# A Mamba-2 scan followed by a maxout FFN: blocks of one chunk from all four batches, decay exponents broadcast from DRAM, scan matmuls in array tiles

## The chip, the cores and the metric

The kernel runs on one core of a Trainium2 chip. The metric is the device time of one execution in microseconds; the time before is the median of three runs.

## The reference

```python
# x (4, 8, 768, 32), a (4, 8, 768), B and C (4, 8, 768, 16): batch, head, token, width
log_a = log(clip(a, 1e-6, 1))
for each chunk of 32 tokens:
    cum = cumsum(log_a of the chunk)
    L = exp(cum[i] - cum[j]) where i >= j, else 0
    y = ((C @ B.T) * L) @ x + (C @ state) * exp(cum)
    state = exp(sum(log_a)) * state + sum_j B_j x_j exp(cum[-1] - cum_j)
X = y as (batch * token, head * 32)          # 3072 x 256
h = max(X @ w1, X @ w2, X @ w3)              # 256 -> 768
out = h @ w_out                              # 768 -> 256
```

All inputs of the scan are float32; the weights come as float64. The result does not depend on the length of the chunk, and both kernels use chunks of 128 tokens, six per batch.

## The kernel before

**Units of work.** There are 24 chunks (4 batches by 6 chunks, batch by batch), each with all 8 heads. Four chunks in a row make a block of 512 tokens, and there are six blocks. For a block the FFN runs in pieces: six of `up` (L330 to L345; three weight matrices, two matmuls of 512 columns each, the maximum formed by a ScalarE copy `m` and two VectorE maxima into `h`) and four of `down` (L347 to L360).

**Scan of a chunk, in four steps.** `scan_inputs` (L225) multiplies C and B by decays (`Cd`, `Bd`), transposes B, Cd and C on PE, and writes C by head with zeros elsewhere (`CT`). It also builds `W` on GpSimd: the log decays where k <= i. `scan_decay` (L254) lets PE form the exponents, `lower` times `W` (`d`, L260, two matmuls of 512 columns), takes the exponential on ScalarE (L263) and masks on GpSimd (L264). It also makes the new state from one matmul `A` (L270). `scan_scores` (L281) multiplies B with `CT` (`s`, L286, two matmuls of 512 columns over the full array) and `L` (L289). `scan_out` (L292) adds the state's share (L302, full array) and the chunk's own (L308, eight matmuls in 32-column tiles) and copies to `yT`.

**What one trace row of PE is.** A float32 matmul that isn't a transpose leaves two records in the trace; 48 matmuls `d` are 96 records.

**Order.** The steps of the next block's scan are spread among the FFN pieces of the current one (the loops at L364 to L382). Tile's scheduler then orders each engine's instructions; engines work in order and wait on semaphores. SP's queue loads the raw tensors (L94) and stores results (L359); ScalarE's queue loads the weights (L110). Twelve weight jobs are decoded from float64 by six VectorE passes, two GpSimd passes and one ScalarE pass each (L106 to L145), the first ones ahead of the first `up`. Eight completion semaphores are used in turn by the loads and stores, so an issue also waits for the DMA that used its semaphore before it, as a rule the eighth ahead; this holds before and after the change.

Of the kernel before, what the change touches and what calls it, by code (L numbers as in the profile page):

```python
# [18 lines left out]
def kernel(  # L19
# [30 lines left out]
    NF = DF // P  # L50
    BLK = 512
    CPB = BLK // P
    NBLK = T // BLK
# [12 lines left out]
    raw = ctx.enter_context(tc.tile_pool(name="raw", bufs=5))  # L66
    att = ctx.enter_context(tc.tile_pool(name="att", bufs=2))
    ffn = ctx.enter_context(tc.tile_pool(name="ffn", bufs=2))
    wraw = ctx.enter_context(tc.tile_pool(name="wraw", bufs=3))
    wtmp = ctx.enter_context(tc.tile_pool(name="wtmp", bufs=2))  # L70
    ps = ctx.enter_context(tc.tile_pool(name="ps", bufs=1, space=PSUM))

    def att_bank(shape, name):
        return ps.tile(shape, FP32, tag="att", bufs=3, name=name)
# [11 lines left out]
    chunks = {}  # L86

    def load(n):
        b, c = divmod(n, NC)
        sl = slice(c * P, (c + 1) * P)  # L90
        st = chunks[n] = {}
        for name, src, w in (("B", B, N), ("C", C, N), ("x", x, D)):
            st[name] = raw.tile([P, NH, w], FP32, tag="raw_" + name, name="raw_" + name)
            nc.sync.dma_start(out=st[name], in_=src[b, :, sl, :].rearrange("h s n -> s h n"))  # L94

    for n in range(CPB):
        load(n)
# [8 lines left out]
    def decoded(dst, src):  # L106
        """dst [P, 2, WCOL] float32 from src [P, 2, WCOL * 2] words of float64s, low word first."""
        shape = [P, 2 * WCOL]
        rb = wraw.tile([P, 2, WCOL, 2], U32, tag="rb", name="rb")
        nc.scalar.dma_start(out=rb.rearrange("p k f w -> p k (f w)"), in_=src)  # L110
        lo, hi = (rb.rearrange("p k f w -> p (k f) w")[:, :, j] for j in range(2))

        def temp(dtype, name):
            return wtmp.tile(shape, dtype, tag=name, name=name)

        # power of two, with the sign: below float32's range 0, above it infinite
        e = temp(U32, "w_e")
# [45 lines left out]
    for o in range(0, NF, 2):  # L163
# [6 lines left out]
    ident = const.tile([P, P], FP32, name="ident")  # L170
    make_identity(nc, ident)
    upper = const.tile([P, P], FP32, name="upper")
    make_upper_triangular(nc, upper, 1.0, diag=True)
    lower = const.tile([P, P], FP32, name="lower")
    make_lower_triangular(nc, lower, 1.0, diag=False)
    ones = const.tile([P, P], FP32, name="ones")
    nc.vector.memset(ones, 1.0)
    # hsel[p, h] = 1 where p, as (head, state), is of head h
# [7 lines left out]
        base=N - 1, channel_multiplier=-1)  # L186

# [5 lines left out]
    tp = att_bank([P, 2, R], "la_tp")  # L193
    for w in range(2):
        nc.tensor.transpose(out=tp[:, w], in_=lr[:, w], identity=ident[0:R, 0:R])
    la = const.tile([P, NB, NH, NC], FP32, name="la")
    nc.vector.tensor_copy(
        out=la.rearrange("p b h c -> p (b h c)"), in_=tp.rearrange("p w r -> p (w r)"))

    def decays(tri, name):  # L200
        d = att_bank([P, NB, NH, NC], name + "_ps")
        nc.tensor.matmul(
            out=d.rearrange("p b h c -> p (b h c)"), lhsT=tri,
            rhs=la.rearrange("p b h c -> p (b h c)"), start=True, stop=True)
        e = const.tile([P, NB, NH, NC], FP32, name=name)
        nc.scalar.activation(e, d, AF.Exp)
        return e

    to_i = decays(upper, "to_i")
    from_j = decays(lower, "from_j")  # L210
    whole = decays(ones, "whole")
    picked = const.tile([HN, NB, NC, NH], FP32, name="picked")
    for b in range(NB):
        nc.vector.tensor_tensor(
            out=picked[:, b], in0=whole[:, b].rearrange("p h c -> p c h"),
            in1=hsel.unsqueeze(1).to_broadcast([HN, NC, NH]), op=ALU.mult)
    full = const.tile([HN, NB * NC], FP32, name="full")
    nc.vector.tensor_reduce(
        out=full, in_=picked.rearrange("p b c h -> p (b c) h"), op=ALU.add, axis=AX.X)

# [191 lines left out]
```

## Time and profile before

| quantity | value |
|---|---|
| median of 3 runs | 415.1 us (415.0 to 415.52) |
| span of the profiled execution | 413.1 us |
| PE busy | 385.2 us, 93% |
| VectorE busy | 199.7 us, 48% |
| GpSimd, ScalarE busy | 86.1 and 83.5 us |
| DMA traffic | 16.09 MB in 81635 packets |

The span runs from the first to the last instruction of the profiled execution; the runs' median is 2.0 us longer, which lies outside the span. A busy PE means that matmuls are in flight, not that the array runs at its peak. Engine waits are put down to what released them.

### The profile page before, as it was taken

The page shows a single profiled execution, that of the slowest core. Times are in us where ns is not written, and L with a number is a line of the kernel's source. Part 1 is how long each engine was busy: PE and PEld are TensorE (multiplying, and loading weights), DVE is VectorE, ACT ScalarE, POOL GpSimd, SP SyncE. Part 2 cuts the span into 40 slices and gives each one's busy share as a digit, 9 for nine tenths or more (in the row PEclk, how much of TensorE's full clock was granted, in tenths as well). Part 3 has the DMA queues.
Part 4 walks back from the last instruction along what each step waited for, and adds up shares of the span by engine and source line. Part 5 has one row for each costly group of instructions (what it writes and reads, how often), then busy time and mean ns, then how long its engine had stood idle before and what let it go on. Part 6 is the DMA issues. An engine that isn't in the chain of part 4 may idle for free.

```text
span 413.1 us, 4050 instructions
## 1 busy us (share of the span) xinstructions
PE 385.2 (93%) x1496; PEld 210.0 (51%) x1496; DVE 199.7 (48%) x308; ACT 83.5 (20%) x161; POOL 86.1 (21%) x109
## 2 busy tenths in 40 slices
PE   0779799599999999999999999999999999999996
PEld 0434343246644446754446754446654456754465
DVE  4999999954334364134454334442334452212220
ACT  2323331211222112222112222022221021211101
POOL 3656554612201012201022201022111021000000
PEclk9999999799999999999999999999999999999999
DMA  8963543011121021231020231020110000000001
GB/s 200 179 108 41 131 117 100 9 18 22 43 51 13 2 25 11 49 55 13 2 25 9 44 63 13 1 28 0 40 38 0 0 2 0 25 27 0 0 2 51
DMA packets 81635, 16.09 MB, mean 39 GB/s; under 512 B 75280, under 2 KB 78544, under 8 KB 81616
## 3 DMA queue, kind: packets, MB, share of 16 engines
q1 hardware_dynamic: 78352, 9.54, 15.2%
q10 hardware_dynamic: 3264, 6.29, 4.9%
q8 instruction: 12, 0.20, 0.2%
q14 instruction: 7, 0.06, 0.1%
HBM read 12.68 MB, written 3.15 MB: 38 GB/s over the span
## 4 chain that ended last, share of the span: by engine, by line
PE 81%; DVE 14%; SPq 2%; issue 1%; DMA 1%; ACT 0%; ACTq 0%; DVEq 0%
PE up L337 41%; PE o L352 16%; PE d L260 8%; PE s L286 8%; PE y L308 3%; SPq L94 2%; PE tr L244 2%; PE y L302 2%; PE A L270 2%; DVE w_m L141 2%; DVE M L289 2%; DVE w_p L132 1%; DVE CT L250 1%; DVE w_s L124 1%; DVE w_e L118 1%
## 5 line engine op out<-in xcount | busy, mean ns | idle before, releaser
L337 PE MATMUL up<-yT,w 128*128 128x512 f32 x432 | 192.5, 599 | 1.4 <-DVE h L344 1.0
L337 PEld LDWEIGHTS up<-yT,w 128*128 128x128 f32 x432 | 82.0, 192 | 101.7 <-issue 94.9
L264 POOL TENSOR_SCALAR_AFFINE_SELECT L<-L 128x512 f32<-128x512 f32 x48 | 32.5, 678 | 205.3 <-ACT L L263 205.2
L352 PE MATMUL o<-wo,h 128*128 128x256 f32 x288 | 66.6, 383 | 0.0
L344 DVE TENSOR_TENSOR m<-m,up 128x512 f32<-128x512 f32 x36 | 24.7, 686 | 77.3 <-PE up L337 77.3
L352 PEld LDWEIGHTS o<-wo,h 128*128 128x128 f32 x288 | 53.9, 190 | 11.5 <-issue 4.9
L289 DVE TENSOR_TENSOR M<-s,L 128x512 f32<-128x512 f32 x48 | 32.9, 689 | 42.3 <-PE s L286 42.3
L260 PE MATMUL d<-W,lower 128*128 128x512 f32 x96 | 48.2, 616 | 2.3 <-ACT L L263 1.0
L263 ACT ACTIVATE L<-d 128x512 f32<-128x512 f32 x48 | 28.5, 596 | 89.1 <-PE d L260 85.0
L286 PE MATMUL s<-CT,BCT 128*128 128x512 f32 x96 | 46.1, 601 | 0.0
L342 ACT COPY m<-up 128x512 f32<-128x512 f32 x36 | 21.1, 586 | 108.3 <-PE up L337 101.7
L344 DVE TENSOR_TENSOR h<-m,up 128x512 f32<-128x512 f32 x36 | 24.7, 686 | 30.7 <-PE up L337 30.7
L230 POOL TENSOR_SCALAR_AFFINE_SELECT W<-la 128x1024 f32<-128x1024 f32 x24 | 27.7, 1155 | 42.6 <-PE d L260 41.9
L250 DVE TENSOR_TENSOR CT<-tr,hsel 128x1024 f32<-128x1024 f32 x24 | 29.2, 1218 | 9.4 <-ACT BCT L247 9.4
L260 PEld LDWEIGHTS d<-W,lower 128*128 128x128 f32 x96 | 18.2, 198 | 21.6 <-issue 15.5
L286 PEld LDWEIGHTS s<-CT,BCT 128*128 128x128 f32 x96 | 17.5, 190 | 15.5 <-issue 12.6
L274 DVE TENSOR_TENSOR S<-A,hsel 128x256 f32<-128x256 f32 x20 | 8.4, 422 | 26.8 <-PE A L270 26.8
L308 PE MATMUL y<-M,raw_x 128*32 128x128 f32 x384 | 16.7, 280 | 2.4 <-DVE M L289 2.3
L247 ACT COPY BCT<-tr 128x256 f32<-128x256 f32 x24 | 8.9, 372 | 35.3 <-PE y L302 30.4
L235 DVE TENSOR_TENSOR Cd<-raw_C,to_i 128x128 f32<-128x128 f32 x24 | 11.0, 458 | 7.7 <-PE tr L244 7.7
L302 PEld LDWEIGHTS y<-BCT,S 128*128 128x128 f32 x80 | 11.6, 191 | 5.8 <-issue 5.7
L277 DVE SCALAR_TENSOR_TENSOR S<-S,full 128x256 f32<-128x256 f32 x16 | 14.5, 904 | 0.0
(54 smaller groups left out, 198.6 us busy)
## 6 DMA issues: line engine op xcount, KB each, us to landing
rb<-in_moe_w_dram ACTq DMA_DIRECT2D x9, 512.0 KB, 4.1
raw_x<-in_x_dram SPq DMA_DIRECT2D x24, 128.0 KB, 2.9
out_dram<-ob SPq DMA_DIRECT2D x12, 256.0 KB, 2.1
raw_B<-in_B_dram SPq DMA_DIRECT2D x24, 64.0 KB, 2.4
raw_C<-in_C_dram SPq DMA_DIRECT2D x24, 64.0 KB, 3.0
rb<-in_moe_w_out_dram ACTq DMA_DIRECT2D x3, 512.0 KB, 3.8
a_sb<-in_a_dram SPq DMA_DIRECT2D x1, 96.0 KB, 2.6
```

The source lines that it names most:

```text
L230: nc.gpsimd.affine_select(out=W, in_=la[:, b, :, c].unsqueeze(2).to_broadcast([P, NH, P]), pattern=[[0, NH], [1, P]], compare_op=ALU.is_ge ...
L250: nc.vector.tensor_tensor(out=CT, in0=tr[:, 2].unsqueeze(1).to_broadcast([HN, NH, P]), in1=hsel.unsqueeze(2).to_broadcast([HN, NH, P]), op ...
L260: nc.tensor.matmul(out=d.rearrange("j h i -> j (h i)"), lhsT=lower, rhs=st["W"][:, g:g + 4].rearrange("k h i -> k (h i)"), start=True, sto ...
L263: nc.scalar.activation(L[:, g:g + 4], d, AF.Exp)
L264: nc.gpsimd.affine_select(out=L[:, g:g + 4], in_=L[:, g:g + 4], pattern=[[0, 4], [1, P]], compare_op=ALU.is_ge, fill=0.0, base=0, channel_ ...
L286: nc.tensor.matmul(out=s.rearrange("j h i -> j (h i)"), lhsT=st["T"][:, 0], rhs=st["CT"][:, g:g + 4].rearrange("p h i -> p (h i)"), start= ...
L289: nc.vector.tensor_tensor(out=M[:, g:g + 4], in0=s, in1=st["L"][:, g:g + 4], op=ALU.mult)
L308: nc.tensor.matmul(out=y[q * D:(q + 1) * D, t], lhsT=st["x"][:, h], rhs=st["M"][:, h], start=(c == 0 and t == 0), stop=True, tile_position ...
L337: nc.tensor.matmul(out=p, lhsT=w_sb[i][:, k, f * P:(f + 1) * P], rhs=yT[blk][:, k], start=(k == 0), stop=(k == KD - 1))
L342: nc.scalar.copy(out=m, in_=p)
L344: nc.vector.tensor_tensor(out=m if i == 1 else hT[blk][:, f], in0=m, in1=p, op=ALU.max)
L352: nc.tensor.matmul(out=o[:, t % 2], lhsT=hT[blk][:, f, t * P:(t + 1) * P], rhs=wo_sb[:, f], start=(f == 0), stop=(f == NF - 1), skip_group ...
```

## The change

- **Blocks.** A block is one chunk of 128 tokens from each of the four batches (512 tokens again), so that the scan of a block handles four batches at once, and the state moves from block to block.
- **Decay.** VectorE forms the cumulative sum `cum` of the log decays in rows, SP writes it to a DRAM tile `cums` and reads it back, each row to all 128 partitions (`L`, four DMAs of 512 KB per block) and each head's row to 16 partitions (`E`, eight DMAs). GpSimd masks with -30000, ScalarE takes the exponential head by head with minus cum as bias. The matmuls `d` and the tiles `W` go.
- **Array tiles.** `s` becomes 16 matmuls per block in 32-row tiles with two heads in each; `A` 16 matmuls in 32-column tiles; the state's share of `y` 16 matmuls in tiles of 32 rows by 64 columns.
- **Weights.** All loads go through SP; four VectorE passes per job in place of six, one more on ScalarE.
- **Order.** PE's order is now the order of the code; the other engines are ordered by the scheduler.

```diff
-    BLK = 512
+    BLK = NB * P
...
-        nc.scalar.dma_start(out=rb.rearrange("p k f w -> p k (f w)"), in_=src)
+            nc.sync.dma_start(out=rb.rearrange("p k f w -> p k (f w)"), in_=src)
...
+    for w in range(2):
+        nc.vector.tensor_tensor_scan(
+            out=cum[:, w], data0=keep, data1=lr[:, w], initial=0.0,
+            op0=ALU.mult, op1=ALU.add)
+    cums = dram.tile([NB, NH, NC, P], FP32, name="cums")
+    nc.sync.dma_start(
+        out=cums.rearrange("b h c s -> (b h c) s").rearrange("(w r) s -> r w s", w=2), in_=cum)
...
+    def decay_load(c):
+        Ls[c] = L = att.tile([P, NB, NH, P], FP32, tag="L", name="L")
+        for b in range(NB):
+            nc.sync.dma_start(out=L[:, b], in_=cums[b, :, c, :].partition_broadcast(P))
+        if c > 0:
+            st = blocks[c]
+            st["E"] = E = raw.tile([HN, NB, P], FP32, tag="E", name="E")
+            for h in range(NH):
+                nc.sync.dma_start(
+                    out=E[h * N:(h + 1) * N], in_=cums[:, h, c, :].partition_broadcast(N))
+
+    def decay_exp(c, b, h0):
+        L = Ls[c]
+        for h in range(h0, h0 + NH // 2):
+            nc.scalar.activation(
+                L[:, b, h], L[:, b, h], AF.Exp, bias=ncum[:, b, h, c:c + 1], scale=1.0)
...
+        if c > 0:
+            E = st["E"]
+            nc.scalar.activation(E, E, AF.Exp)
+            st["Cd"] = Cd = att.tile([HN, NB, P], FP32, tag="Cd", name="Cd")
+            nc.vector.tensor_tensor(out=Cd, in0=trC, in1=E, op=ALU.mult)
...
+    def scan_scores(c, b0):
+        st = blocks[c]
+        L = Ls[c]
+        banks = [att_bank([P, 2, 2, P], "s") for _ in range(NP)]
+        for i in range(2):
+            b = b0 + i
+            for r in range(NP):
+                rows = slice(r * PN, (r + 1) * PN)
+                nc.tensor.matmul(
+                    out=banks[r][:, i].rearrange("j g i -> j (g i)"), lhsT=st["BT"][rows, b],
+                    rhs=st["CT"][rows, b].rearrange("p g i -> p (g i)"),
+                    start=(i == 0), stop=True, tile_position=(r * PN, 0), skip_group_check=True)
+        for r in range(NP):
+            M = L[:, b0:b0 + 2, 2 * r:2 * r + 2]
+            nc.vector.tensor_tensor(out=M, in0=banks[r], in1=M, op=ALU.mult)
...
+    order = tc.manual_schedule(engines=tc_pe)
...
+    for c in range(NC):
+        n = c + 1
+        scan = {0: (scan_in, n), 1: (scan_state, n), 2: (scan_scores, n, 0),
+                4: (scan_scores, n, 2), 6: (scan_out, n)}
+        for k, (g, i) in enumerate(pieces):
+            g(c, i)
+            for _ in range(2):
+                decode()
+                fetch()
+            if n < NC and k in scan:
+                scan[k][0](*scan[k][1:])
+            if k == 0 and n + 1 < NC:
+                load(n + 1)
+            if k == 3 and n + 1 < NC:
+                decay_load(n + 1)
+            if 4 <= k < 8 and n + 1 < NC:
+                b = k - 4
+                decay_mask(n + 1, b)
+                for h0 in range(0, NH, NH // 2):
+                    decay_exp(n + 1, b, h0)
```

The start of SP's queue, before: the inputs of the four chunks of block 0, with no weights between them.

```order
L81 DMA a_sb<-in_a_dram 96x2x128
L94 DMA raw_B<-in_B_dram 128x8x16
L94 DMA raw_C<-in_C_dram 128x8x16
L94 DMA raw_x<-in_x_dram 128x8x32
L94 DMA raw_B<-in_B_dram 128x8x16
```

The start of SP's queue after the change (`rb` are the undecoded weights):

```order
L86 DMA a_sb<-in_a_dram 96x2x128
L98 DMA raw_B<-in_B_dram 128x32x16
L98 DMA raw_C<-in_C_dram 128x32x16
L98 DMA raw_x<-in_x_dram 128x32x32
L136 DMA rb<-in_moe_w_dram 128x2x512 x3
L210 DMA cums<-cum 96x2x128
L136 DMA rb<-in_moe_w_dram 128x2x512 x2
L234 DMA L<-cums 128x8x128 x4
L136 DMA rb<-in_moe_w_dram 128x2x512 x4
L98 DMA raw_B<-in_B_dram 128x32x16
L98 DMA raw_C<-in_C_dram 128x32x16
```

The store of `cums` now stands behind the raw tensors and three weights, its broadcast `L` behind two more, and four weights stand between that and the raw tensors of the next block.

VectorE ahead of the first block's output, before, around the products `M` of the last chunk of block 0:

```order
L289 TENSOR_TENSOR M<-s,L 128x512
L129 TENSOR_SCALAR w_p<-w_e 128x512
L289 TENSOR_TENSOR M<-s,L 128x512
L132 TENSOR_TENSOR w_p<-w_p,w_s 128x512
L141 SCALAR_TENSOR_TENSOR w_m<-rb,w_tf 128x512
```

The same place after the change, where the product is written over `L`:

```order
L328 TENSOR_TENSOR L<-s,L 128x2x256 x4
L152 TENSOR_SCALAR w_e<-rb 128x512
L159 TENSOR_SCALAR w_t<-rb 128x512
L152 TENSOR_SCALAR w_e<-rb 128x512
L159 TENSOR_SCALAR w_t<-rb 128x512
L328 TENSOR_TENSOR L<-s,L 128x2x256 x4
```

The first passes on two weights, which need their loads, now stand between the first and the last four products of block 0.

ScalarE in the first FFN block, before (`m` is the copy of an `up` result, `L<-d` the exponential):

```order
L263 ACTIVATE L<-d 128x512
L342 COPY m<-up 128x512
L139 ACTIVATE w_tf<-w_t 128x512
L110 DMA rb<-in_moe_w_dram 128x2x512
L342 COPY m<-up 128x512
```

The same place after the change:

```order
L371 COPY m<-up 128x512
L166 ACTIVATE w_p<-w_e 128x512
L163 ACTIVATE w_tf<-w_t 128x512
L166 ACTIVATE w_p<-w_e 128x512
L276 COPY BT<-trB 128x512
L280 ACTIVATE CT<-trC,parity 128x4x128 x2
L251 ACTIVATE L<-L,ncum 128x128 x32
L283 ACTIVATE E<-E 128x512
L371 COPY m<-up 128x512
```

Between the copies of the first and the second `up` now stand all 32 exponentials of the next block and that of `E`.

## Rows read from the trace of the kernel before

**Rows 1.** The page's busy times: engine, us (share of the span), instructions.

```profile
PE 385.2 (93%) x1496; PEld 210.0 (51%) x1496; DVE 199.7 (48%) x308; ACT 83.5 (20%) x161; POOL 86.1 (21%) x109
```

**Rows 2.** Stretches: us, busy us (instructions) per engine, granted clock, DMA share, GB/s.

```profile
core 0: us, PE busy (x) PEld busy (x) DVE busy (x) ACT busy (x) POOL busy (x), PEclk, DMA share, GB/s
0.00:46.80 46.80, 29.12 (x141) 15.26 (x142) 40.24 (x68) 13.41 (x27) 24.73 (x37) 1.00 0.68 129
46.80:118.20 71.40, 65.44 (x248) 34.98 (x247) 51.13 (x84) 16.34 (x31) 26.27 (x27) 0.95 0.27 60
73.90:79.00 5.10, 0.15 (x2) 0.00 (x0) 5.10 (x9) 1.60 (x3) 2.67 (x3) 0.84 0.01 2
79.50:87.02 7.52, 7.52 (x15) 3.21 (x13) 5.72 (x11) 1.21 (x2) 3.71 (x4) 0.69 0.20 20
180.87:243.57 62.70, 62.70 (x250) 34.44 (x248) 26.92 (x41) 12.35 (x24) 9.30 (x12) 1.00 0.17 26
367.84:413.10 45.26, 41.53 (x120) 22.71 (x120) 8.25 (x12) 4.68 (x8) 0.00 (x0) 0.99 0.03 12
```

**Rows 3.** PE in order of time, first block: start us, us, line, operation.

```profile
46.81 10.46 PE L337 MATMUL up<-yT,w 128*128 128x512 f32 x24
...
79.54 7.64 PE L337 MATMUL up<-yT,w 128*128 128x512 f32 x12
87.02 0.61 PE L302 MATMUL y<-BCT,S 128*128 128x128 f32 x4
```

**Rows 4.** PE in order of time, a middle block.

```profile
192.78 5.32 PE L337 MATMUL up<-yT,w 128*128 128x512 f32 x12
197.94 1.88 PE L286 MATMUL s<-CT,BCT 128*128 128x512 f32 x4
199.65 5.31 PE L337 MATMUL up<-yT,w 128*128 128x512 f32 x12
...
207.06 0.27 PE L244 MATMUL tr<-ident,Cd 128*128 128x128 f32 x1
207.17 0.27 PE L244 MATMUL tr<-ident,raw_C 128*128 128x128 f32 x1
...
225.13 0.61 PE L302 MATMUL y<-BCT,S 128*128 128x128 f32 x4
225.68 0.64 PE L308 MATMUL y<-M,raw_x 128*32 128x128 f32 x16
226.25 2.86 PE L352 MATMUL o<-wo,h 128*128 128x256 f32 x12
```

**Rows 5.** Groups by line: shapes, count, busy us, mean ns, idle before and releasers.

```profile
L289 DVE TENSOR_TENSOR M<-s,L 128x512 f32<-128x512 f32 x48 | 32.9, 689 | 42.3 <-PE s L286 42.3
L263 ACT ACTIVATE L<-d 128x512 f32<-128x512 f32 x48 | 28.5, 596 | 89.1 <-PE d L260 85.0 <-DMA rb<-in_moe_w_out_dram 2.9 <-DVE M L289 1.2
L342 ACT COPY m<-up 128x512 f32<-128x512 f32 x36 | 21.1, 586 | 108.3 <-PE up L337 101.7 <-DVE S L277 5.1 <-DVE w_e L118 1.5
L230 POOL TENSOR_SCALAR_AFFINE_SELECT W<-la 128x1024 f32<-128x1024 f32 x24 | 27.7, 1155 | 42.6 <-PE d L260 41.9 <-DVE la L197 0.6
L247 ACT COPY BCT<-tr 128x256 f32<-128x256 f32 x24 | 8.9, 372 | 35.3 <-PE y L302 30.4 <-PE tr L244 5.0
L135 DVE TENSOR_SCALAR w_t<-rb 128x512 uint32<-128x512 uint32 x12 | 7.5, 626 | 0.0
L118 DVE TENSOR_SCALAR w_e<-rb 128x512 uint32<-128x512 uint32 x12 | 6.3, 527 | 2.5 <-DMA rb<-in_moe_w_dram 2.5
```

**Rows 6.** DMA queues from 0 to 17.2 us: packets, MB, share of 16 engines.

```profile
q1 hardware_dynamic: 12592, 1.14, 54.0%
q10 hardware_dynamic: 1088, 2.10, 38.3%
```

**Rows 7.** DMA queue of SP from 0.8 to 4 us.

```profile
q1 hardware_dynamic: 208, 0.10, 11.1%
```

**Rows 8.** DMA issues of the page: KB each, median us from issue to landing.

```profile
out_dram<-ob SPq DMA_DIRECT2D x12, 256.0 KB, 2.1
```

More of the change, by code (lines that the diff above doesn't have):

```diff
@@ L38 @@
     nc = tc.nc
+    tc_pe = {nc.tensor.engine}
     NB, NH, S, D = x.shape
@@ L84, with load @@
     )
-    chunks = {}
-    def load(n):
-        b, c = divmod(n, NC)
+    blocks = {}
+    def load(c):
         sl = slice(c * P, (c + 1) * P)
-        st = chunks[n] = {}
+        st = blocks[c] = {}
         for name, src, w in (("B", B, N), ("C", C, N), ("x", x, D)):
[L93 to L97, printed above, removed]
+            st[name] = raw.tile([P, BH, w], FP32, tag="raw_" + name, name="raw_" + name)
+            nc.sync.dma_start(
+                out=st[name], in_=src[:, :, sl, :].rearrange("b h s n -> s (b h) n"))
+    load(0)
     w_sb = [const.tile([P, KD, DF], FP32, name="w%d" % i) for i in range(3)]
@@ L170 @@
+    for _ in range(3):
+        fetch()
     ident = const.tile([P, P], FP32, name="ident")
     make_identity(nc, ident)
[L172 to L177, printed above, removed]
     hsel = const.tile([HN, NH], FP32, name="hsel")
@@ L186 @@
         base=N - 1, channel_multiplier=-1)
+    parity = const.tile([HN, 2], FP32, name="parity")
+    nc.vector.tensor_reduce(
+        out=parity, in_=hsel.rearrange("p (r g) -> p g r", g=2), op=ALU.add, axis=AX.X)
+    keep = const.tile([R, P], FP32, name="keep")
+    nc.vector.memset(keep, 1.0)
     nc.vector.tensor_scalar(
@@ L192 @@
     nc.scalar.activation(lr, a_sb, AF.Ln)
-    tp = att_bank([P, 2, R], "la_tp")
+    cum = const.tile([R, 2, P], FP32, name="cum")
     for w in range(2):
[L195 to L207, printed above, removed]
@@ new lines, in scan_out @@
+    def scan_out(c):
+        st = blocks[c]
+        M = Ls[c]
+        yT[c] = ffn.tile([P, KD, BLK], FP32, tag="yT", name="yT")
+        ys = [att_bank([P, NB, P], "y") for _ in range(KD)]
+        if c > 0:
+            Sp = states[c]
+            for b in range(NB):
+                for r in range(NP):
+                    rows = slice(r * PN, (r + 1) * PN)
+                    q = r % 2 * 2 * D
+                    nc.tensor.matmul(
+                        out=ys[r // 2][q:q + 2 * D, b],
+                        lhsT=Sp[rows, b].rearrange("p g d -> p (g d)"), rhs=st["Cd"][rows, b],
+                        start=(b == 0), stop=False, tile_position=(r * PN, q),
+                        skip_group_check=True)
+        for b in range(NB):
+            for h in range(NH):
+                t, q = divmod(h, QH)
@@ L312, in scan_out @@
[L312 to L324 removed]
+            nc.scalar.copy(out=yT[c][:, t], in_=ys[t].rearrange("p b i -> p (b i)"))
     hT = {}
[L328 removed]
@@ L364 @@
[L364 to L381 removed]
+                    out=m if i == 1 else hT[c][:, f], in0=m, in1=p, op=ALU.max)
@@ new lines, in down @@
+    def down(c, u):
+        o = ffn_bank([P, 2, DM], "o")
+        for i in range(2):
+            b = 2 * u + i
+            for f in range(NF):
+                nc.tensor.matmul(
+                    out=o[:, i], lhsT=hT[c][:, f, b * P:(b + 1) * P], rhs=wo_sb[:, f],
+                    start=(f == 0), stop=(f == NF - 1), skip_group_check=True)
+        ob = ffn.tile([P, 2, DM], FP32, tag="ob", bufs=3, name="ob")
+        nc.scalar.copy(out=ob, in_=o)
+        nc.sync.dma_start(
+            out=out.rearrange("(b s) m -> s b m", s=S)[c * P:(c + 1) * P, 2 * u:2 * u + 2],
+            in_=ob)
@@ new lines @@
+    order = tc.manual_schedule(engines=tc_pe)
+    ctx.enter_context(order)
+    decay_load(0)
+    ncum = by_token(cum, "ncum", -1.0)
+    from_j = by_token(fj, "from_j", 1.0)
+    for b in range(NB):
+        decay_mask(0, b)
+        for h0 in range(0, NH, NH // 2):
+            decay_exp(0, b, h0)
+    scan_in(0)
+    for _ in range(3):
+        fetch()
+    scan_state(0)
+    scan_scores(0, 0)
+    scan_scores(0, 2)
+    for _ in range(3):
+        decode()
+        fetch()
+    load(1)
+    decay_load(1)
```

307 lines of the change are left out of this document (128 added, 179 removed).

## Prediction

> **What bounds the kernel now.** I read the busy shares first: the tensor engine (PE) is busy for 93% of the span, VectorE for 48% [rows 1]. Then the stretches: a middle block of 512 tokens lasts 62.7 us with PE busy for all of it, and the last block, which has no scan beside it, has 41.5 us of PE work and 45.3 us to the end of the span [rows 2]. So a block is 41.3 us of FFN (without the last drain of 0.2) and 62.7 - 41.3 = 21.4 us of scan. PE bounds the middle blocks: a scan microsecond taken off PE counts there in full, until another engine is late. Ahead lies a head of 46.8 us until the first `up` [rows 3], with the DMA engines 68% busy and PE only 29.1 us [rows 2].
>
> **PE per block before.** The order of PE's rows shows the price of each kind. Four records of `s` (two matmuls) take 199.65 - 197.94 = 1.71 us [rows 4], 0.428 for a record of 512 columns, and hence 0.214 for 256, 0.107 for 128, 0.053 for 64. A block holds 16 records of `s` and 16 like them of `d`: 6.85 us each. Transposes, `A` and `y` make up the other 7.7.
>
> **PE per block after.** `d` goes: -6.85. What stays, each with its bounds:
> - Eight transposes at 0.11 us (207.17 - 207.06) [rows 4]: 0.9.
> - `y` within a chunk: eight matmuls in 32-column tiles, 16 records of 128 columns, take 226.25 - 225.68 = 0.57 us [rows 4]. One after the other they would take 1.71, four side by side 0.43. So column tiles do run side by side, and a visit to them costs 0.15 for going in and out. 64 records at 0.027: 1.7.
> - `A`, 32 records of 64 columns in 32-column tiles: 0.43 if four run side by side, 0.85 at the 0.027 per record that `y` reaches. I take 0.85, the nearest row.
> - `s`, 32 records of 256 columns in 32-row tiles. No row shows a row tile. Below: four side by side, 32 x 0.214 / 4 = 1.7. Above: no overlap at all, 6.85. In between: each record brings its own weights of 128 columns, and records with such weights follow each other no closer than 0.11 us (the transposes) [rows 4]; 32 x 0.11 = 3.5. I take 2.6, midway between side by side and that pace.
> - `y` from the state, 32 records of 128 columns in 32-row, 64-column tiles: 0.86 to 1.7, 3.4 with no overlap. I take 1.3.
> - Five visits to tiles at 0.15: 0.7.
>
> Sum 8.0 us, where the favourable ends give 6.3, the slow weights 9.3 and no overlap 15.2. The period becomes 41.3 + 8.0 = 49.3 us, four times.
>
> A rule speaks for the slow end: the Trainium skill (TensorE: Matmul & The Clock Gate, LDWEIGHTS) says that a weight load takes its time by columns and not by rows, so that 32 rows by 128 columns load no faster than a full array. By that rule `s` takes 3.5 us and the period is 50.6; by rows that run side by side it is 47.6. The 0.11 us between transposes, with 128 weight columns each, agree with it for a full array [rows 4]; no row loads 32 rows.
>
> **Cover in the middle blocks.** The exponentials move to one head each: 32 per block on ScalarE. A 512-column one takes 596 ns, a 256-column copy 372 [rows 5]; the slope gives 0.27 us at 128 columns, so 8.6 us, and with eight 512-column passes and six `m` copies at 0.59 beside them about 17 of 49 us. VectorE loses `CT`, `Cd`, `Bd` in small pieces and keeps 12 maxima and 8 `M` products at 0.69 [rows 5]: 15 us. GpSimd gets four masks of 1.16 [rows 5], `Bd` and the state: about 8. The DMA engines: 12288 packets of 64 to 128 bytes at 11.8 ns (54% of 16 x 17.2 us over 12592) [rows 6] are 9.1 us on 16 engines, as before; new are 4096 packets of 512 bytes for `L`. The rows of the first 3.2 us hold 208 packets, most of them such: 11.1% x 16 x 3.2 / 208 = 27 ns [rows 7], so 7.0 us, and 0.9 for `E`. About 19 of 49 us. Nothing here is late: each `L` is loaded a block ahead. I cost all of it at nothing; it would cost once the loads of a block pass 49 us.
>
> **The head.** Now the decay takes a round trip through DRAM, and one queue (SP's) carries everything. Ahead of `cums` stand block 0's raw tensors and three weights. Before, the same raw bytes and four weights took 17.2 us of nearly full DMA [rows 6]; a weight is 272 packets of 97 ns on 16 engines, 1.65 us. So `cums` moves at 15.5 and lands at 17.4, given the 2.1 us of a store [rows 8]. Two weights are ahead of `L`: 18.8. Four parts of `L`, 7.0: 25.8, landed by 26.3. Mask and exponentials of the last part end at 29.6. VectorE is later: in its order, `w_e` and `w_t` of two weights stand ahead of the last four `M` products, and these weights are queued behind `L`: landed by 30.0, then 1.2 us [rows 5], then 4 x 0.69: 34.0. The last `y` and the first `yT` copy: 36.0 for the first `up`, where 46.8 stands before. VectorE is spared two of six passes per weight, which is why decoding does not hold this longer.
>
> **Block 0.** It has 41.3 us of FFN and 8.0 of scan, of which `A` is hidden in a wait: 7.2. PE has idled in the head; after the wait at 73.9 to 79.0 twelve records of `up` took 87.02 - 79.54 = 7.5 us in place of 5.16 at a granted clock of 0.69 (between the levels of 1.2 and 2.4 GHz) [rows 2 to 4]. I charge this twice, 4.7. Then a new wait. ScalarE's order puts all 32 exponentials of the next block and `E` ahead of the `m` copy of the second `up`, and VectorE puts `Cd`, which needs `E`, ahead of its maxima. DMA: four weights to 32.4, raw tensors to 41.5, `L` to 49.0, the last piece of `E`, whose issue waits for the eighth DMA ahead of it, a part of `L`, 51.1. Mask 50.2, eight exponentials 52.3, `E` 52.9, copy 53.5. PE is at 36.0 + 7.5 + 1.1 + 5.2 = 49.7: it waits 3.8 us. The next `L` holds the fourth `m` copy in the same way, 1.2 us by the same count (68.8 against 67.6). Block 0: 41.3 + 7.2 + 4.7 + 5.0 = 58.2, where 71.4 stands before [rows 2].
>
> **The sum.** 36.0 + 58.2 + 4 x 49.3 + 45.3 = 336.7 us of span against 413.1. The runs' median is 2.0 above the span, which I keep: 339.
>
> **Rivals.**
> - Weight loads one after another, as worked out above: 9.3 per scan, 5 x 1.3 = 6.5 more: 345. For it: the 0.14 us per record of `y` from the state now (0.55 for four, 225.13 to 225.68), where the stream needs 0.107 [rows 4]. Against it: `y` in column tiles, near its stream's rate. Chance 0.20.
> - Row tiles that do not overlap, so that the change does not do what it says on PE: 15.2 per scan, 36 more: 375. Column tiles speak against it, nothing shows rows. Chance 0.07.
> - Reading the same eight rows of `cums` for 128 partitions at half rate: 7 us more for each of the first three `L`, all on the path of the head and of block 0, hidden afterwards: 360. No row of before reads the same bytes again and again. Chance 0.13.
> - The other side: these reads bind the whole kernel. Until the last `L` lands the rest of the queue takes about 94 us (the head's 17, nine weights 15, five sets of raw tensors 46, `E` with its gaps 10, stores 6), and what follows it 75 (30 left of block 4, then 45); with 2 us outside the span and T for each of six `L` the time is 171 + 6T. It is slower than before from T = 41 us, 5.8 times the 7.0 of the row's rate; at 7 times, 49 us, the time is 465. Against it: the packet prices by size lie near one line (12, 27, 97 ns for about 90, 512 and 2048 bytes) [rows 6, 7]. Chance 0.04.
>
> **How the numbers follow.** The forecast keeps 0.56. Its own bounds: the scans between 6.3 and 9.3 (-8 to +7), the head 4 either way, block 0's waits gone or doubled (-5 to +5): 325 to 353. To leave out no more than 2 in 10 the range takes in the half-rate reads: 322 to 364; row tiles without overlap (0.07), bound reads (0.04) and some misjudged start (0.07) are left out. All cases but the last rival are faster: 0.95, same 0.01, slower 0.04, with 0.2% as what a measurement can tell.
>
> **What would show it.** Right: first `up` near 36 us; a middle block near 49 with PE busy throughout; `s` rows spaced under 0.11 us; waits on `E` or `L` only in block 0. Wrong: `L` parts far over 1.75 us each; `s` rows 0.2 apart; `m` copies late behind exponentials in later blocks.

## The result and the profile after

The changed kernel takes **342.4 us** (median of four runs, 342.15 to 343.07) against 415.3: ratio 0.825, 95% interval 0.8236 to 0.8264. 339 was predicted, with a range of 322 to 364. The profiled execution took 342.15, its span is 340.4. Executions of one kernel can fall into two groups some per cent apart, the longer ones at a lower granted clock; ratios are those of the shorter ones.

The page's span and busy times after; the line of PE answers to [rows 1]:

```profile
span 340.4 us, 4340 instructions
PE 300.3 (88%) x1668; PEld 172.0 (51%) x1668; DVE 123.4 (36%) x185; ACT 119.3 (35%) x303; POOL 64.9 (19%) x70
```

PE has 85 us less to do and still ends the span. Where the 73 us went is read from the stretches, with the columns of [rows 2]: head, block 0, the idle time and the cold `up` in it, the first middle block, the block without a next state, the last block.

```profile
0.00:40.76 40.76, 14.14 (x141) 9.93 (x141) 26.93 (x44) 22.47 (x55) 21.43 (x28) 1.00 1.08 236
40.76:101.54 60.78, 51.17 (x289) 28.73 (x289) 31.55 (x43) 32.91 (x90) 25.90 (x25) 0.92 0.75 143
52.70:62.40 9.70, 0.09 (x9) 0.01 (x1) 0.92 (x2) 9.64 (x32) 2.75 (x4) 0.72 1.21 164
62.40:70.09 7.69, 7.69 (x12) 3.13 (x13) 7.61 (x11) 2.89 (x5) 5.53 (x6) 0.69 1.16 304
101.54:150.12 48.58, 48.58 (x290) 27.78 (x289) 14.27 (x22) 17.25 (x46) 6.77 (x7) 1.00 0.44 82
247.27:295.07 47.80, 47.80 (x257) 27.37 (x256) 13.92 (x21) 7.52 (x13) 0.00 (x0) 1.00 0.04 12
295.07:340.40 45.33, 41.42 (x121) 22.61 (x119) 8.26 (x12) 5.28 (x9) 0.00 (x0) 1.00 0.05 18
```

| stretch, us | before | predicted | after |
|---|---|---|---|
| head, to the first `up` | 46.8 | 36.0 | 40.8 |
| block 0 | 71.4 | 58.2 | 60.8 |
| blocks 1 to 4, sum | 249.6 | 197.2 | 193.5 |
| last block | 45.3 | 45.3 | 45.3 |

The sum of blocks 1 to 4 before is 413.1 less the other rows; after, three blocks take 48.58 each and the fourth 47.80. So 56 of the 73 us come from the middle blocks, 17 from the start.

PE in order of time in a middle block after, the counterpart of [rows 4]:

```profile
106.69 0.60 PE L271 MATMUL trB<-ident,raw_B 128*128 128x128 f32 x4
...
112.81 0.65 PE L295 MATMUL A<-raw_x,Bd 128*32 128x64 f32 x32
113.39 5.42 PE L366 MATMUL up<-yT,w 128*128 128x512 f32 x12
118.74 1.15 PE L322 MATMUL s<-CT,BT 32*128 32x256 f32 x16
119.82 10.57 PE L366 MATMUL up<-yT,w 128*128 128x512 f32 x24
...
141.92 1.10 PE L341 MATMUL y<-Cd,S 32*64 32x128 f32 x32
142.95 1.96 PE L349 MATMUL y<-L,raw_x 128*32 128x128 f32 x64
144.83 5.45 PE L381 MATMUL o<-wo,h 128*128 128x256 f32 x24
```

From one start to the next, 16 records of `s` take 1.08 us (0.067 each), twice a block; `y` from the state takes 1.03, `y` within the chunk 1.88, `A` 0.58.

Two stretches of ScalarE in order of time after, the end of the head and the wait in block 0:

```profile
27.78 2.45 ACT L251 ACTIVATE L<-L,ncum 128x128 f32<-128x128 f32 x8
30.98 7.12 ACT L251 ACTIVATE L<-L,ncum 128x128 f32<-128x128 f32 x24 [0.76 <-POOL L L244]
...
51.91 9.45 ACT L251 ACTIVATE L<-L,ncum 128x128 f32<-128x128 f32 x32 [3.27 <-POOL L L244]
61.26 0.61 ACT L283 ACTIVATE E<-E 128x512 f32<-128x512 f32 x1
61.78 0.56 ACT L371 COPY m<-up 128x512 f32<-128x512 f32 x1
```

The third `up` starts at 62.40, when the `m` copy of the second has been made. That copy stands behind 32 exponentials and `E` of the next chunk. VectorE's last four products of the head:

```profile
36.44 2.48 DVE L328 TENSOR_TENSOR L<-s,L 128x512 f32<-128x512 f32 x4 [0.44 <-issue]
```

GpSimd, in the same stretches:

```profile
23.14 1.41 POOL L174 TENSOR_TENSOR w<-w_m,w_p 128x512 f32<-128x512 f32 x1 [0.62 <-DVE w_m L172]
25.61 0.91 POOL L155 TENSOR_SCALAR w_e<-w_e 128x512 uint32<-128x512 uint32 x1 [1.05 <-DVE w_e L152]
26.59 1.16 POOL L244 TENSOR_SCALAR_AFFINE_SELECT L<-L 128x1024 f32<-128x1024 f32 x1
27.71 1.73 POOL L174 TENSOR_TENSOR w<-w_m,w_p 128x512 f32<-128x512 f32 x1
...
49.54 1.29 POOL L174 TENSOR_TENSOR w<-w_m,w_p 128x512 f32<-128x512 f32 x1 [1.23 <-DVE w_m L172]
50.79 4.21 POOL L244 TENSOR_SCALAR_AFFINE_SELECT L<-L 128x1024 f32<-128x1024 f32 x4
```

SyncE's issues of `L`, of chunk 0 and then of chunk 1 (count, shortest, median and longest issue in ns, first and last start), and their times to landing:

```profile
L234 SPq DMA_DIRECT2D L<-cums x4: 367/1027/2188, 15.9 to 18.5; - x4
...
DMA to landing us min/median/max: 4.9/6.9/8.0
...
L234 SPq DMA_DIRECT2D L<-cums x4: 861/1990/2611, 35.0 to 40.8; - x4
...
DMA to landing us min/median/max: 7.1/7.9/8.0
```

Of chunk 0 the first part is on the chip at 15.9 + 4.9 = 20.8 and the last at 18.5 + 8.0 = 26.5, but the first mask starts at 26.59. Of chunk 1 the first part is there at 35.0 + 8.0 = 43.0 at the latest, the last at 48.8, but no mask starts before 50.79. Both times GpSimd's queue has passes on weights ahead of the masks, and these passes wait for VectorE's decoding.

### The profile page after: what moved, and what is told of

Same layout as the page of the kernel before. It is cut to its first block, busy times and chain, and to the rows that moved or that the text cites. A ratio compares the mean times of both kernels' runs of the same rounds, so it can differ in the third digit from the quotient of the medians.

```text
span 340.4 us, 4340 instructions
## 1 busy us (share of the span) xinstructions
PE 300.3 (88%) x1668; PEld 172.0 (51%) x1668; DVE 123.4 (36%) x185; ACT 119.3 (35%) x303; POOL 64.9 (19%) x70
## 4 chain that ended last, share of the span: by engine, by line
PE 81%; SPq 7%; DMA 4%; ACT 3%; DVE 2%; issue 1%; POOL 0%; ACTq 0%; POOLq 0%
PE up L366 53%; PE o L381 19%; SPq L98 5%; PE s L322 3%; PE y L349 3%; ACT L L251 3%; DMA L<-cums 2%; SPq L234 2%; PE y L341 2%; DMA rb<-in_moe_w_dram 1%; SPq L136 1%; DVE w_p L168 1%; DVE w_e L152 1%; DVE w_m L172 1%; DMA E<-cums 1%
## 5 line engine op out<-in xcount | busy, mean ns | idle before, releaser
L366 PE MATMUL up<-yT,w 128*128 128x512 f32 x432 | 193.5, 602 | 10.1 <-ACT m L371 9.6
L251 ACT ACTIVATE L<-L,ncum 128x128 f32<-128x128 f32 x192 | 57.7, 390 | 8.4 <-POOL L L244 8.4
L244 POOL TENSOR_SCALAR_AFFINE_SELECT L<-L 128x1024 f32<-128x1024 f32 x24 | 26.6, 1119 | 98.5 <-DMA L<-cums 98.4
L322 PE MATMUL s<-CT,BT 32*128 32x256 f32 x192 | 17.6, 446 | 17.0 <-DVE L L328 17.0
L328 DVE TENSOR_TENSOR L<-s,L 128x512 f32<-128x512 f32 x48 | 29.8, 684 | 6.0 <-PE s L322 3.8
L322 PEld LDWEIGHTS s<-CT,BT 32*128 32x128 f32 x192 | 11.4, 206 | 26.3 <-DVE L L328 17.7
L168 DVE SCALAR_TENSOR_TENSOR w_p<-rb,w_p 128x512 uint32<-128x512 uint32 x12 | 15.0, 1252 | 0.5 <-ACT w_p L166 0.4
L349 PE MATMUL y<-L,raw_x 128*32 128x128 f32 x384 | 13.5, 296 | 0.8 <-DVE L L328 0.8
L174 POOL TENSOR_TENSOR w<-w_m,w_p 128x512 f32<-128x512 f32 x9 | 12.9, 1429 | 7.0 <-DVE w_p L168 5.0
L349 PEld LDWEIGHTS y<-L,raw_x 128*32 128x32 f32 x384 | 11.3, 119 | 2.9 <-DVE L L328 1.3
L172 DVE SCALAR_TENSOR_TENSOR w_m<-rb,w_tf 128x512 f32<-128x512 uint32 x12 | 10.5, 876 | 0.0
L285 DVE TENSOR_TENSOR Cd<-trC,E 128x512 f32<-128x512 f32 x5 | 3.5, 692 | 19.2 <-ACT CT L280 10.6
```

Source lines behind the costliest of these rows:

```text
L168: nc.vector.scalar_tensor_tensor(out=power, in0=hi, scalar=0x80000000, in1=power, op0=ALU.bitwise_and, op1=ALU.bitwise_or)
L172: nc.vector.scalar_tensor_tensor(out=mant, in0=lo, scalar=2.0 ** -52, in1=topf, op0=ALU.mult, op1=ALU.add)
L244: nc.gpsimd.affine_select(out=L[:, b], in_=L[:, b], pattern=[[0, NH], [1, P]], compare_op=ALU.is_ge, fill=MASKED, base=0, channel_multipli ...
L251: nc.scalar.activation(L[:, b, h], L[:, b, h], AF.Exp, bias=ncum[:, b, h, c:c + 1], scale=1.0)
L322: nc.tensor.matmul(out=banks[r][:, i].rearrange("j g i -> j (g i)"), lhsT=st["BT"][rows, b], rhs=st["CT"][rows, b].rearrange("p g i -> p ( ...
L328: nc.vector.tensor_tensor(out=M, in0=banks[r], in1=M, op=ALU.mult)
```

## The experiments

**Theory:** the middle blocks are bound by PE and shortened by tiles and by the missing `d`; what the start lost against the prediction (4.8 us in the head, 2.6 in block 0) are places in the queues of ScalarE and GpSimd. **Rivals:** the transfers or VectorE's decoding set the start, or the row tiles save nothing.

**Block 0's order alone.**

```diff
-    for b in range(NB):
-        decay_mask(1, b)
-        for h0 in range(0, NH, NH // 2):
-            decay_exp(1, b, h0)
...
+            if c == 0 and k == 1:
+                scan_cd(1)
...
+            if c == 0 and k in (1, 2):
+                for b in (2 * k - 2, 2 * k - 1):
+                    decay_mask(1, b)
+                    for h0 in range(0, NH, NH // 2):
+                        decay_exp(1, b, h0)
```

> Order alone: block 0's exponentials of chunk 1 are written after its second and third up, E and Cd of chunk 1 after the second. Theory 'queue order' (the 9.6 us before the third up come from the m copy standing behind 32 exponentials and E on ScalarE): the third up waits at most 2 us and runs at full clock, 12 us go, of which 2 to 6 may come back as waits before s or on maxima behind decoding: 332 to 336 us against 342.4. Rival 'transfers': the last parts of L and E land at 48.7 and 50.8 whatever the order, and what follows them (masks, 9.5 us of exponentials, products) ends as late as before, so the wait moves to s or y of chunk 1: 340 to 343 us.

Measured: 336.7 us, ratio to before 0.8106 (0.8086 to 0.8125). ScalarE now takes the copies between the exponentials:

```profile
52.06 0.99 ACT L251 ACTIVATE L<-L,ncum 128x128 f32<-128x128 f32 x3 [2.85 <-POOL L L244]
52.95 0.56 ACT L378 COPY m<-up 128x512 f32<-128x512 f32 x1
53.42 5.36 ACT L251 ACTIVATE L<-L,ncum 128x128 f32<-128x128 f32 x18
58.69 0.57 ACT L378 COPY m<-up 128x512 f32<-128x512 f32 x1
```

Block 0 goes from 60.8 to 54.9 us with the same transfers and the same work. So the wait of 9.6 us was a place in ScalarE's queue. Part of it comes back: PE waits 0.49 for `m`, 2.30 for a maximum and 1.70 before the first `down`, somewhat more than was allowed for, so that the time stands 0.7 above the expected range. For block 0 the transfers' rival falls.

**`L` by matmul again.**

```diff
-            nc.sync.dma_start(out=L[:, b], in_=cums[b, :, c, :].partition_broadcast(P))
...
+        nc.gpsimd.affine_select(
+            out=W, in_=la[:, b, :, c].unsqueeze(2).to_broadcast([P, NH, P]),
+            pattern=[[0, NH], [1, P]], compare_op=ALU.is_ge, fill=0.0,
+            base=0, channel_multiplier=-1)
...
+        nc.tensor.matmul(
+            out=d.rearrange("j h i -> j (h i)"), lhsT=lower,
+            rhs=Ws[c, b][:, h0:h0 + 4].rearrange("k h i -> k (h i)"), start=True, stop=True)
+        nc.scalar.activation(L[:, b, h0:h0 + 4], d, AF.Exp)
+        nc.gpsimd.affine_select(
+            out=L[:, b, h0:h0 + 4], in_=L[:, b, h0:h0 + 4], pattern=[[0, 4], [1, P]],
+            compare_op=ALU.is_ge, fill=0.0, base=0, channel_multiplier=-1)
...
-    scan_out(0)
     for b in range(NB):
         decay_mask(1, b)
         for h0 in range(0, NH, NH // 2):
             decay_exp(1, b, h0)
+    scan_out(0)
```

> The broadcast alone undone: L comes from eight 512-column matmuls per block with the lower triangle, eight 512-column exponentials and masks behind them; E still comes through DRAM, tiles and chunks stay. Theory of the prediction: d costs PE 6.85 us in each of four blocks, a middle block goes from 48.6 to 55.4 us, +27.4; the head loses 7 us of transfers and 32 short exponentials, so the first up comes at 33 to 37 in place of 40.8, and block 0's wait of 9.6 and its cold up go, -12: 342.4 + 27.4 - 6 - 12 = 352, range 348 to 358. Rival 'd is free': PE has slack in a middle block, the period stays under 50 us: 325 to 330. Rival 'the head is bound by decoding, not by L': first up at 40 or later, wait stays: 366 to 370.

Measured: 378.8 us (three of four executions; the fourth took 425.7), ratio 0.9115 (0.9092 to 0.9137), above every expectation. The stretches are head, block 0 and a middle block; the rows under them are GpSimd's costliest groups in the head.

```profile
0.00:55.18 55.18, 31.66 (x172) 15.25 (x172) 35.84 (x50) 23.45 (x43) 40.35 (x51) 0.81 0.84 161
55.18:116.75 61.57, 57.80 (x305) 31.29 (x305) 27.36 (x38) 16.94 (x30) 26.15 (x27) 0.97 0.31 48
116.75:172.24 55.49, 55.49 (x306) 30.74 (x304) 14.26 (x22) 12.93 (x22) 11.45 (x15) 1.00 0.23 34
```

```profile
L261 POOL TENSOR_SCALAR_AFFINE_SELECT L<-L 128x512 f32<-128x512 f32 x16 | 13.3, 842 | 1.6 <-ACT L L260 1.4
L249 POOL TENSOR_SCALAR_AFFINE_SELECT W<-la 128x1024 f32<-128x1024 f32 x8 | 9.5, 1194 | 2.9 <-DVE la L226 2.5 <-PE d L257 0.3
```

The middle block is right to 0.1 us: 55.49 against 48.58, so `d` costs 6.91 where 6.85 was computed. The head is wrong by 20 and block 0 by 6 (61.6, where 60.8 + 6.85 - 12 = 55.6 was expected). In the head, two chunks of `W` and of masks (22.8 us) and the weights (8.3 and 6.3 for products and `w_e`) fill GpSimd, 40.35 of 55.18. I had reckoned with the transfers that go and not with the selects that come. But half of the selects are those of chunk 1, and this run also writes chunk 1's `d` ahead of `scan_out(0)` in PE's order:

```profile
39.44 8.28 PE L257 MATMUL d<-W,lower 128*128 128x512 f32 x12
...
50.06 1.95 PE L360 MATMUL y<-L,raw_x 128*32 128x128 f32 x64
```

From 39.44 to 50.06 PE's queue is held by that `d`, with the first block's `y` behind it. So the 14.4 us by which the head is longer than the changed kernel's are in part this run's own order. What the broadcast is worth there is not shown; shown are the 6.9 us a block on PE, 20.7 in blocks 1 to 3.

**One row tile.** Every `s` reads the first 32 rows of its operands in the first tile.

```diff
-                    out=banks[r][:, i].rearrange("j g i -> j (g i)"), lhsT=st["BT"][rows, b],
-                    rhs=st["CT"][rows, b].rearrange("p g i -> p (g i)"),
-                    start=(i == 0), stop=True, tile_position=(r * PN, 0), skip_group_check=True)
+                    out=banks[r][:, i].rearrange("j g i -> j (g i)"), lhsT=st["BT"][0:PN, b],
+                    rhs=st["CT"][0:PN, b].rearrange("p g i -> p (g i)"),
+                    start=(i == 0), stop=True, tile_position=(0, 0), skip_group_check=True)
```

> Every s matmul reads the first 32 rows of its operands and uses the first row tile, so scores of the other heads are not computed (those of the first pair stand in their place); number, shapes and order of the matmuls stay. Theory 'row tiles run side by side': 32 records of 256 columns take 32 x 0.214 = 6.85 us per block in place of 2.15, +4.7 in each of blocks 0 to 4, the head's hidden: 342.4 + 19 to 24 = 361 to 366. Rival 'a 32-row matmul is short by itself': no change, 342. Rival 'only the weight loads overlap': records at about 0.11 us, +1.4 per block: 348 to 350.

Measured: 379.3 us as the median of four (three from 379.1 to 380.5, the shortest 373.2), more than expected. PE in order of time in a middle block of the profiled execution (it took 379.5), then the stretch of these 16 with the columns of [rows 2]:

```profile
127.13 3.72 PE L322 MATMUL s<-CT,BT 32*128 32x256 f32 x16
130.78 12.26 PE L366 MATMUL up<-yT,w 128*128 128x512 f32 x24
```

```profile
127.13:130.85 3.72, 3.72 (x18) 2.96 (x17) 1.88 (x3) 0.63 (x1) 0.00 (x0) 1.00 0.00 0
```

16 records in one tile take 3.65 us from start to start, 0.228 each, at a granted clock of 1.00, and in four tiles 1.08: a gain of 3.4 times, 5.1 us a block and 25.7 in blocks 0 to 4. That makes 368. The shortest execution took 5 us more, and what these are is not shown, since the kept trace is of another.

**The same tiles in another order.** The loops over `r` and `i` in `scan_scores` change places, so that two matmuls of one row tile follow each other.

```diff
-        for i in range(2):
-            b = b0 + i
-            for r in range(NP):
+        for r in range(NP):
+            for i in range(2):
+                b = b0 + i
```

> The same s matmuls in another order: two batches in one row tile after another, then the next row tile. By the run with one row tile a record takes 0.232 us alone and 0.072 in turns over four tiles. Theory 'neighbours overlap only when they are in different row tiles': two of four run side by side, 16 records in about 1.9 us in place of 1.15, +1.5 in each of blocks 0 to 4: 349 to 350. Rival 'the order does not matter, the array keeps four going': 342 to 343. Rival 'no overlap at all across a change of tile': 16 records in 3.7, 355 or more.

Measured: 343.2 us, ratio 0.8256 (0.8232 to 0.828), no difference from the changed kernel's; 16 records take 1.10 from start to start (119.89 to 120.99):

```profile
119.89 1.17 PE L322 MATMUL s<-CT,BT 32*128 32x256 f32 x16
120.99 1.55 PE L366 MATMUL up<-yT,w 128*128 128x512 f32 x3
```

So two matmuls (four records) of one row tile in a row do not lengthen the 16, and strict turns over the tiles are not needed. The first theory falls, its first rival holds.

**`L` twice.** The load of each part of chunks 3 to 5 stands in a loop of two.

```diff
-            nc.sync.dma_start(out=L[:, b], in_=cums[b, :, c, :].partition_broadcast(P))
+            for _ in range(2 if c > 2 else 1):
+                nc.sync.dma_start(out=L[:, b], in_=cums[b, :, c, :].partition_broadcast(P))
```

> Each part of L is loaded twice for chunks 3 to 5 (blocks 1 to 3), the head and block 0 unchanged: 7 us more of DMA in a block of 48.6 whose DMA share is 0.44. Theory 'hidden': L is loaded a block ahead, middle blocks stay at 48.6, 342.4 within 0.7. Rival 'the broadcast contends with the other transfers or with the engines' reads': a middle block grows by 2 us or more, 348 or more.

Measured: 344.2 us, ratio 0.8286 (0.8269 to 0.8304). Blocks 1 to 3 take 49.08, 49.51 and 48.94, 1.8 more in all, and the first `up` comes 0.8 later, at 41.6. Twelve more transfers of half a megabyte are nearly hidden, though not within the 0.7 us that was allowed; the rival's 2 us a block do not show.

**Earlier transfers, three ways.** First, `cums` and the first `L` on ScalarE's DMA queue:

```diff
-    nc.sync.dma_start(
+    nc.scalar.dma_start(
         out=cums.rearrange("b h c s -> (b h c) s").rearrange("(w r) s -> r w s", w=2), in_=cum)
...
+            q = nc.scalar if c == 0 else nc.sync
+            q.dma_start(out=L[:, b], in_=cums[b, :, c, :].partition_broadcast(P))
```

> cums and the four parts of the first L alone go on ScalarE's DMA queue. Theory 'queue order': the parts land some 6 us earlier, but GpSimd and ScalarE take the work in an order that changes with it: the next chunk's exponentials come ahead of the yT copies, so the first up comes no earlier (43 to 47), and the wait in block 0 shrinks by about as much: 337 to 345. Rival 'the head ends with its transfers': first up at 35, wait as before: 336.

Measured: 348.3 us, ratio 0.8379 (0.8347 to 0.841), slower than the changed kernel: the first `up` comes at 49.9. The transfers did not come earlier as a whole. The first part lands at 7.4 + 6.6 = 14.0, but the last at 11.8 + 16.3 = 28.1, where it was 26.5 in the changed kernel, and GpSimd waits for it:

```profile
23.56 1.09 POOL L245 TENSOR_SCALAR_AFFINE_SELECT L<-L 128x1024 f32<-128x1024 f32 x1 [2.74 <-DMA L<-cums]
28.17 1.09 POOL L245 TENSOR_SCALAR_AFFINE_SELECT L<-L 128x1024 f32<-128x1024 f32 x1 [3.52 <-DMA L<-cums]
```

ScalarE's order changed more than was foreseen, too: `BT` and `CT` now stand behind all 32 exponentials, so the first `s` waits for `CT` until 33.4. Second, with the order of block 0 beside it (the first and second diff together):

> The early broadcast and the order of block 0 together, the engines' order otherwise left to the scheduler. Theory 'queue order': 19 exponentials of chunk 1 still stand ahead of the yT copies (9 us of ScalarE with the weights between), so the first up comes near 42, block 0 as in the run with its order alone (54.9): 335 to 340. Rival 'the gains add up' (the parts land 6 us earlier and the first up with them): 330 or 331.

Measured: 350.8 us, ratio 0.8436 (0.84 to 0.8473); first `up` at 49.5, block 0 58.5: worse than both theories, the gains do not add up. Here the last part lands at 10.6 + 17.8 = 28.4. Third, everything in a written order, on all engines:

```diff
+    tc_pe = {e.engine for e in (nc.tensor, nc.scalar, nc.vector, nc.gpsimd, nc.sync)}
...
+        q = nc.scalar if c == 0 else nc.sync
...
+                if 1 <= k < 5:
+                    decay(1, k - 1)
```

> All five engines follow an order written out: cums and the first L go on ScalarE's queue ahead of most weights, only three weights are made before the first up, each mask and its eight exponentials of the first L follow its part, the exponentials of chunk 1 go eight at a time behind the m copies, each weight is made in two stages so that no engine waits inside it. Theory 'queue order' (the head's extra 5 us and the 9.6 us are both places in a queue, not transfers or work): first L landed by about 20, first up at 29 to 33, no wait over 2 us in block 0, middle blocks 48.6 as before: 342.4 - 8 to 12 - 10 = 318 to 325. Rival 'transfers': head and block 0 together are bound by 54 us of DMA for what comes before the first down, so the wait only moves: 332 or more. Rival 'VectorE': decoding (3.4 us a weight), maxima and products take about 46 us of block 0's 50, so up waits for maxima there: 325 to 332.

Measured: 374.6 us, ratio 0.9015 (0.8987 to 0.9044); first `up` at 49.7, block 0 82, where 318 to 325 us were expected. Two reasons can be read. ScalarE in order of time:

```profile
8.85 14.53 ACTq L247 DMA_DIRECT2D L<-cums  x4
23.42 0.58 ACT L296 COPY BT<-trB 128x512 f32<-128x512 f32 x1 [17.82 <-DMA raw_x<-in_x_dram]
```

The four issues hold ScalarE for 14.5 us, and nothing behind them in its queue runs. They start at 8.9, 9.3, 12.9 and 23.0 and take 0.4 to 0.6 us each; the rest is waiting for a completion semaphore that an earlier transfer still has: the third for a weight that lands at 12.9, the fourth for `raw_x`, issued at 9.4 and landed 13.6 us later, at 23.0. The last part so lands at 23.0 + 6.2 = 29.2. And in block 0 the stages of a weight wait for one another through four engines that each follow a written order, with `m` copies and maxima behind them: PE waits five times, 19.6 us in all, for `m`. In none of the three runs does the last part of the first `L` land earlier than in the changed kernel, so none of them shows what earlier transfers would give.

**Only the order of the loads.** No transfer leaves SyncE; that queue is written out, the engines that compute stay with the scheduler. The order of block 0 from the first experiment is in it too, and `A`, `E` and `Cd` of chunk 1 come behind later `up` pieces.

```diff
+    tc_pe = {nc.tensor.engine, nc.sync.engine}
...
+    load(0, "BC")
...
+    fetch()
...
     nc.sync.dma_start(
         out=cums.rearrange("b h c s -> (b h c) s").rearrange("(w r) s -> r w s", w=2), in_=cum)
+    fetch()
+    fetch()
...
+    decay_load(0)
+    load(0, "x")
```

> No DMA leaves SyncE's queue; only its order is written out, and the places of a few steps beside the order of block 0: one weight ahead of cums, two more ahead of the first L, raw_x and the second three weights behind it; in block 0 L of chunk 1 ahead of the third three weights, its A after the fourth up, E and Cd after the fifth. VectorE, ScalarE and GpSimd stay with the scheduler, which now puts three weights in place of five ahead of the first 32 exponentials and none between them and the yT copies. Theory 'queue order' (head): first L landed by 20, its exponentials done by 31, first up at 33 to 35 in place of 40.8, block 0 50 to 55: 323 to 331 us. Rival 'the head cannot be shortened by order': first up at 39 or later, 335 to 338. Rival 'given back in block 0': first up at 33 to 35, but weights and products late there, block 0 at 58 or more: 333 to 338.

Measured: 340.2 us (median of six, 338.0 to 343.7), ratio 0.8163 (0.8141 to 0.8185), where 323 to 331 were expected. In this run `A` of chunk 1 takes the bank from which `Cd` is still to be made, so values of `Cd` differ; number and shapes of the instructions stay. The head comes out as the theory has it, first `up` at 32.7. Block 0 takes 56.4, where 50 to 55 were expected, and blocks 1 to 3 lose 5.5, 2.5 and 2.9 us, which no theory had. In block 1 ScalarE waits 7.76 us for masks and then holds the `m` copy behind 25 exponentials, since `L` now lands too late there. With that mended (`Cd` first, `L` right behind the raw tensors, ScalarE and GpSimd in written order from block 1 on):

```diff
-            if k == 3 and n + 1 < NC:
+            if k == min(c, 1) ^ 1 and n + 1 < NC:
                 decay_load(n + 1)
...
+        if c == 1:
+            ctx.enter_context(tc.manual_schedule(
+                engines={nc.scalar.engine, nc.gpsimd.engine}))
```

> The run before with three repairs: Cd of chunk 1 ahead of its A, the next chunks' L on SyncE's queue right behind their raw tensors (there they came behind three ups and ScalarE's exponentials, ahead of m copies, waited for them: blocks 1 and 2 took 54.1 and 51.0), and from block 1 on ScalarE and GpSimd in written order, eight exponentials behind each of the fifth m copy to the second output copy. Theory 'queue order': first up 32.7 as there, block 0 56.4 as there (VectorE near full with decoding, maxima and products), blocks 1 to 3 48.6, then 47.8 and 45.3, 1.8 outside the span: 32.7 + 56.4 + 145.7 + 47.8 + 45.3 + 1.8 = 330, range 327 to 333. Rival 'the loads of a block no longer fit beside it': blocks 1 to 3 stay above 50.5: 336 or more.

Measured: **329.4 us**, ratio 0.7935 (0.792 to 0.795), the fastest of all. The profiled execution took 332.07. GpSimd's first mask, ScalarE at the end of its head, then the stretches from the first `up`:

```profile
17.65 1.42 POOL L247 TENSOR_SCALAR_AFFINE_SELECT L<-L 128x1024 f32<-128x1024 f32 x1
...
19.11 2.45 ACT L254 ACTIVATE L<-L,ncum 128x128 f32<-128x128 f32 x8 [0.76 <-POOL L L247]
22.91 7.12 ACT L254 ACTIVATE L<-L,ncum 128x128 f32<-128x128 f32 x24 [1.35 <-POOL L L247]
```

```profile
33.27:91.40 58.13, 53.19 (x289) 29.54 (x289) 38.07 (x54) 36.05 (x96) 30.69 (x29) 0.94 0.76 168
91.40:139.98 48.58, 48.58 (x290) 27.79 (x289) 14.26 (x22) 14.93 (x38) 6.77 (x7) 1.00 0.43 82
```

The first exponential starts 8.7 us earlier than in the changed kernel, and the first `up` comes 7.5 us earlier. Two things do this together. The first part of `L` lands at 10.8 + 5.2 = 16.0, 4.8 us earlier; and its mask starts 1.6 us behind that, where it was 5.8 in the changed kernel, since fewer passes on weights stand ahead of it on GpSimd. No run moves one without the other. The middle blocks are untouched.

## Why the prediction was right

- **PE bounds the middle blocks: right.** PE is busy for all of 48.58 us; 49.3 was predicted. `d` was 6.91 for 6.85. `s`, taken at 2.6 between bounds of 1.7 and 6.85, is 2.16, `y` from the state 1.03 for 1.3, `A` 0.58 for 0.85 (nearer to four side by side), the eight transposes 0.87 for 0.9, `y` 1.88 for 1.7. The FFN parts around the five visits take 0.8 more than the 41.3 us, where 0.7 was charged. The errors nearly cancel.
- **The rule on weight loads:** had loads of 128 columns kept records 0.11 us apart, `s` would have taken 3.5; at 0.067 the trace speaks against that reading for different row tiles. The row that the prediction took it from could not show such a pace: the 0.11 us between transposes is also what their 128 streamed columns take (0.107 by its own price). The Trainium skill (TensorE: Matmul & The Clock Gate, Measured speedup vs the span model) gives 3.07 times for four row tiles of 32 rows and 512 columns; the run with one tile gives 3.65 / 1.08 = 3.4 here, with 256 columns. The slow-load rival and the one without overlap both fall.
- **Cover: right.** VectorE 14.3, ScalarE 17.3, GpSimd 6.8 of 48.6, DMA share 0.44; 15, 17, 8 and 0.39 (19 of 49) were predicted, and `L` twice costs 0.4 to 0.9 a block.
- **The transfers of the head: right.** The first `L` is issued from 15.9 to 18.5 and landed within 8.0 us, by 26.5; 26.3 was predicted. No slow reading of the same rows, so these two rivals fall as well.
- **The rest of the head: the step that failed is "Mask and exponentials of the last part end at 29.6".** It let the exponentials run as the parts land. The parts do land from 20.8 to 26.5, but GpSimd has passes on weights ahead of the first mask (26.59) and puts a weight's product between two masks: the first eight exponentials start at 27.78, the others at 30.98, and all end at 38.1. With masks on time they would end near 31.5 by an estimate from the trace: the first part's at 22.0, then 32 exponentials at 0.297 us (7.12 / 24), which is slower than the parts land. The last product ends at 38.9, where "34.0" stands, and the first `up` follows 1.9 later, as the 2.0 of the text. VectorE's weights, named there as what is late, did not hold the products: they waited for masks and exponentials. But GpSimd's passes ahead of the masks wait for VectorE's decoding in their turn, so as a rival decoding is not ruled out here. The last run's first `up` at 33.3 shows that order sets the head, SyncE's and GpSimd's together; how much is GpSimd's alone is read from the traces and not shown by a run.
- **Block 0: right in kind, wrong in size.** The wait stands where it was put, behind 32 exponentials and `E` on ScalarE, and the `up` behind it is cold (7.69 at 0.69). But "Mask 50.2, eight exponentials 52.3" again took 24 of 32 exponentials as done by then: with every mask late they end at 61.3, so the wait is 9.6 and not 3.8. The first `up` (5.3 us) was not cold, -2.35; [rows 3] had the first `up` of before at 10.46 us for 24 records, not cold either. The second wait did not come, -1.2.

In sum: head +4.8, block 0 +2.6, middle blocks -3.7: 340.4 of span against 336.7. That the total is right to 1% is in part luck, since these errors, and those within block 0, have both signs; what was right in kind is the bound on the middle blocks, the cover and the transfers.

## What to carry to other kernels

When transfers replace matmuls, follow the landed data through every in-order queue: who masks it, what stands ahead of it there, and whose copy stands behind it. The landing time was right to 0.2 us and still the stage ended 5 us later. When a test run puts a removed step back, ask also where that step now stands on the other engines (here GpSimd's selects and PE's own order in the head), or the run measures its order as well. And leave the issue of large transfers to an engine that computes nothing: an issue that waits for an earlier transfer's semaphore holds all the work behind it.

## What the runs showed that I had not expected

- Four `L` issues held ScalarE 14.5 us, nearly all of it waiting for earlier transfers to land, and 6.23 in the run with only these moved, where two of the issues took 3.3 and 1.8 us themselves.
- Row tiles keep their gain when two matmuls of one tile follow each other (1.10 for 1.08 us).
- The first `L` on ScalarE's DMA queue, beside the weights on SyncE's: its first part landed at 14.0 in place of 20.8, its last at 28.1 in place of 26.5.
